# Two attention decodes on one core: the value loads and output weights of the full-cache part move from the SP queue to the Activation queue

## The chip, the cores and the metric

The kernel runs on one core of one Trainium2 chip. The metric is the device time of one execution in microseconds. Times of a kernel are medians of its timed runs; each profile is of one execution, and its span is 1 to 2 us below the time of that execution.

## The reference, cut to what matters

Two decode attentions for the same batch of 4, one query token each, joined on the last axis. A is grouped (32 query heads, 8 key heads) over the last 2048 positions of its cache. B, the "full-cache part", is plain multi-head over all 8192 positions.

```python
def _B_ref(x, k_cache, v_cache, wq, wo):           # k_cache, v_cache: [4, 32, 8192, 128] bf16
    q = (x @ wq).reshape(B, 1, 32, 128).transpose(0, 2, 1, 3)
    scores = einsum("bhqd,bhkd->bhqk", q, k_cache) * 128 ** -0.5
    o = einsum("bhqk,bhkd->bhqd", softmax(scores), v_cache)
    return o.transpose(0, 2, 1, 3).reshape(B, 1, 4096) @ wo
```

B reads 2 x 268 MB of cache once. All the inputs read are 587 MB.

## The kernel before

B is cut into 64 chunks of two heads of one batch entry. A chunk has 4 MB of keys and 4 MB of values; each lands as 128 rows of 32 KB, one for each partition. Keys and values have two buffers each (the last values have one more). For each chunk, TensorE transposes the keys in 16 groups of 8 tiles; VectorE, or in every third group ScalarE (the Activation engine), copies a group from PSUM to SBUF; TensorE multiplies by the query. The value part of the chunk before comes behind the keys of a chunk. Output weights of B (`wos`) are 256 KB in 128 rows of 2 KB, one load for every four chunks.

```python
def keys_part(c):
    for g in range(ch["NG"]):                      # 16 groups
        emit_T(ch["s"] + g)                        # 8 transposes, then a copy on ScalarE if g % 3 == 2
        if g >= SLAG:
            emit_S(ch["s"] + g - SLAG)             # scores
        # [...] at g == 10 of odd chunks: emit_fin, which reads wos and frees it
for c in range(NC):
    # [...]
    keys_part(c)
    values_part(c - 1, c)                          # [...] values of c-1; max and exp of c
```

All big loads stand in one list on the SP queue: keys of chunk c+1, values of c, keys of c+2, and so on. Each waits for its buffer: keys for the last transposes of two chunks earlier, values for the value part of two chunks earlier.

```python
for kind, c in loads:
    if kind == "k" and c >= NCA and (c == NCA or (c - NCA) % 4 == 3 and c > NCA + 3):
        dma_wos((c - NCA) // 4)
    dma_kv(kind, c)
    # [...]
```

The engines' streams are recorded first. Repeated stretches on TensorE, VectorE and ScalarE become loops, if their instructions are the same.

## Time and profile before

| | before |
|---|---|
| median of the timed runs | 1374.2 us (1374.04 to 1374.27) |
| span of the profiled execution | 1372.6 us |
| data moved, mean rate | 587.53 MB, 428 GB/s |
| TensorE busy | 86% |

Three more lines are from the page's list of loads: out<-in, queue, count, size of one, and the median time from issue to landing.

```profile
kv<-in_B_k_cache_dram SPq DMA_DIRECT2D x63, 4096.0 KB, 26.5
kv<-in_B_v_cache_dram SPq DMA_DIRECT2D x63, 4096.0 KB, 30.9
...
wos<-in_B_wo_dram SPq DMA_DIRECT2D x16, 256.0 KB, 20.3
```

Keys and values both land some three load times (9.7 us each) after their issue: the queue is always about three loads deep.

### The profile page before, as it was taken

The numbers are of one execution on the slowest core, as the hardware profiler recorded it, in microseconds if no ns is written. First come the engines' busy times: TensorE is split into PE (matmuls) and PEld (weight loads), VectorE is DVE, ScalarE is ACT, GpSimd is POOL, SyncE is SP. The second block draws the span as 40 slices with busy tenths as digits, with TensorE's granted clock in tenths as the row PEclk, the third lists the DMA queues.
The fourth block names the chain that finished last, engine by engine and source line by source line (L and its number), as shares of the span: only waits on it lengthen the run. The fifth ranks groups of instructions, "written<-read, shape, count | busy, mean of one in ns | idle before, by whom it ended". The sixth has DMA issues, their size and how long they took to land.

```text
span 1372.6 us, 59967 instructions
## 1 busy us (share of the span) xinstructions
PE 1176.5 (86%) x27065; PEld 1132.9 (83%) x27067; DVE 656.6 (48%) x1434; ACT 434.7 (32%) x650; POOL 7.3 (1%) x28
## 2 busy tenths in 40 slices
PE   4888898889888888988888888888898888888888
PEld 4777898888888888888888878888898888888888
DVE  1775454445444444454445444444454444444544
ACT  1553232333223322332233323322333233323322
POOL 2000000000000000000000000000000000000000
PEclk9998999999999999999999999999999999999999
DMA  9999999999999999999999999999999999999998
GB/s 400 423 424 432 429 433 428 433 432 432 432 431 433 429 434 428 434 430 434 430 434 430 430 433 432 432 431 433 429 433 431 434 429 434 430 432 432 432 427 352
DMA packets 25261, 587.53 MB, mean 428 GB/s; under 512 B 2820, under 2 KB 2840, under 8 KB 6296
## 3 DMA queue, kind: packets, MB, share of 16 engines
q1 hardware_dynamic: 25208, 587.22, 99.8%
q8 instruction: 16, 0.26, 0.1%
q14 instruction: 5, 0.04, 0.0%
q10 hardware_dynamic: 32, 0.01, 0.0%
HBM read 587.21 MB, written 0.01 MB: 428 GB/s over the span
## 4 chain that ended last, share of the span: by engine, by line
DMA 65%; PE 33%; issue 1%; DVE 1%; ACT 0%; SPq 0%; DVEq 0%
DMA kv<-in_B_k_cache_dram 57%; PE tr L408 21%; PE sc L410 9%; DMA kv<-in_A_k_cache_dram 5%; DMA kv<-in_B_v_cache_dram 3%; PE po L410 2%; PE fin L410 1%; PE ms L410 0%; ACT kt L476 0%; DVE sA L527 0%; SPq L365 0%; ACT pba L597 0%; PE ms L408 0%; DVE zA L683 0%; DVE rm L536 0%
## 5 line engine op out<-in xcount | busy, mean ns | idle before, releaser
L408 PE MATMUL tr<-identb,kv 128*128 128x128 bf16 x8704 | 697.9, 230 | 148.8 <-DMA kv<-in_B_k_cache_dram 141.5
L478 DVE COPY kt<-tr 128x1024 bf16<-128x1024 bf16 x736 | 502.6, 690 | 457.1 <-PE tr L408 452.7
L408 PEld LDWEIGHTS tr<-identb,kv 128*128 128x128 bf16 x8704 | 552.9, 104 | 165.2 <-DMA kv<-in_B_k_cache_dram 81.7
L476 ACT ACTIVATE kt<-tr 128x1024 bf16<-128x1024 bf16 x352 | 359.3, 1023 | 666.8 <-PE tr L408 666.7
L410 PE MATMUL sc<-qb,kt 128*128 128x64 bf16 x8704 | 446.2, 196 | 14.3 <-ACT kt L476 12.8
L410 PEld LDWEIGHTS sc<-qb,kt 128*128 128x128 bf16 x8704 | 366.4, 100 | 26.0 <-ACT kt L476 20.2
L410 PE MATMUL po<-pbb,kv 128*128 128x64 bf16 x8320 | 284.4, 192 | 4.5 <-issue 3.9
L410 PEld LDWEIGHTS po<-pbb,kv 128*128 128x128 bf16 x8320 | 263.2, 97 | 7.1 <-issue 4.1
L577 ACT ACTIVATE pbb<-sc,negb 64x128 bf16<-64x128 f32 x128 | 51.6, 403 | 254.3 <-DVE negb L564 253.5
L541 DVE TENSOR_REDUCE rm<-sc 64x1 f32<-64x128 f32 x128 | 37.0, 289 | 56.6 <-PE sc L410 55.7
L553 DVE TENSOR_REDUCE gm<-ms 1x2 f32<-1x128 f32 (+1 forms) x72 | 20.1, 279 | 48.4 <-PE ms L408 48.4
L564 DVE COPY negb<-ms 128x1 f32<-128x1 f32 (+1 forms) x72 | 11.4, 158 | 47.0 <-PE ms L410 46.8
L410 PE MATMUL ms<-identf,gx 1*128 1x1 f32 (+1 forms) x144 | 27.2, 256 | 0.8 <-DVE zA L683 0.8
L666 DVE TENSOR_TENSOR oz<-po,rz 128x8 bf16<-128x8 f32 x33 | 5.5, 166 | 40.7 <-PE po L410 40.7
L410 PEld LDWEIGHTS ms<-identf,gx 1*128 1x128 f32 (+1 forms) x144 | 21.1, 182 | 4.6 <-DVE zA L683 0.9
L577 ACT ACTIVATION_READ_ACCUMULATOR pbb<-sc,negb 64x1 f32 x128 | 23.7, 185 | 0.0
L410 PE MATMUL po<-pba,kv 128*128 128x64 bf16 x512 | 20.5, 199 | 3.5 <-issue 2.1
L410 PEld LDWEIGHTS po<-pba,kv 128*128 128x128 bf16 x512 | 17.9, 102 | 5.7 <-ACT pba L597 4.2
L408 PE MATMUL ms<-identf,rm 128*1 128x128 f32 (+1 forms) x72 | 19.5, 271 | 2.4 <-DVE rm L536 2.3
L557 DVE TENSOR_SCALAR gx<-gm 1x128 f32<-1x128 f32 (+1 forms) x72 | 16.0, 222 | 2.5
L683 DVE CAST zB<-ms 64x8 bf16<-64x8 f32 x64 | 10.5, 164 | 9.2 <-PE ms L410 8.7
L410 PE MATMUL ms<-xT,kv 128*128 128x4 bf16 x256 | 7.1, 166 | 8.8 <-DMA kv<-in_A_wq_dram 5.0
(61 smaller groups left out, 173.9 us busy)
## 6 DMA issues: line engine op xcount, KB each, us to landing
kv<-in_B_k_cache_dram SPq DMA_DIRECT2D x63, 4096.0 KB, 26.5
kv<-in_B_v_cache_dram SPq DMA_DIRECT2D x63, 4096.0 KB, 30.9
kv<-in_A_k_cache_dram SPq DMA_DIRECT2D x8, 2048.0 KB, 14.8
kv<-in_A_v_cache_dram SPq DMA_DIRECT2D x8, 2048.0 KB, 16.2
kv<-in_A_wq_dram SPq DMA_DIRECT2D x1, 4096.0 KB, 12.5
kv<-in_B_wq_dram SPq DMA_DIRECT2D x1, 4096.0 KB, 27.1
wor<-in_A_wo_dram SPq DMA_DIRECT2D x8, 512.0 KB, 9.8
wos<-in_B_wo_dram SPq DMA_DIRECT2D x16, 256.0 KB, 20.3
```

What stands on the lines that cost most here:

```text
L408: sch.add("pe", lambda e: e.transpose(o, l, r), waits, key)
L410: sch.add("pe", lambda e: e.matmul(o, l, r, start=start, stop=stop), waits, key)
L476: sch.add("act", lambda e: e.activation(dst, src, ACTF.Copy), waits=waits, key=("ev", s))
L478: sch.add("dve", lambda e: e.tensor_copy(dst, src), waits=waits, key=("ev", s))
L541: sch.add("dve", lambda e, src=src, pp=pp: e.tensor_reduce(out=rm[pp, m, 0:1], in_=src, axis=AX.X, op=ALU.max), waits=[("S", ch["s_last"]) ...
L553: sch.add("dve", lambda e: e.tensor_reduce(out=gm[0:C, m, 0:U], in_=src, axis=AX.X, op=ALU.max), waits=[("trm", c)], key=("gmax", c))
L557: sch.add("dve", lambda e: e.tensor_scalar(out=dst, in0=gv, scalar1=-scale, scalar2=None, op0=ALU.mult), waits=[("gmax", c)], key=("gx", c))
L564: sch.add("dve", lambda e: e.tensor_copy(negb[:, m, 0:C], ms[:, col:col + C]), waits=[("bc", c)], key=("negb", c))
L577: sch.add("act", lambda e, src=src, pp=pp, n=n, u=u: e.activation(probs_of(c)[pp, :, u], src, ACTF.Exp, bias=negb[pp, m, 0:1], scale=scale ...
L666: sch.add("dve", lambda e: e.tensor_tensor(out=o, in0=i0, in1=i1, op=ALU.mult), waits=waits, key=("oT", c))
L683: sch.add("dve", lambda e, src=src, pp=pp: e.tensor_copy(z[pp, :].rearrange("p (r b) -> p r b", r=k), src), waits=[("sm", c)] + free if h ...
```

## The change

The intent is to take values and weights out of the list on SP, so that neither kind waits behind the other's buffer. Values are issued by the Activation engine between its copies: ahead of group 11 of the same chunk's keys (group 2 for the last chunk), with the weights ahead of them in every fourth chunk.

```diff
-            sch.add_dma("sp", lambda e: e.dma_start(wos[...], src), "d_wos",
+            sch.add_dma(VQ if hp else "sp", lambda e: e.dma_start(wos[...], src), "d_wos",
[...]
-            sch.add_dma("sp", lambda e: e.dma_start(dst, src), "d_h%d" % at, waits=waits, key=(kind, c))
+            sch.add_dma("sp" if kind == "k" else VQ, lambda e: e.dma_start(dst, src), "d_h%d" % at, waits=waits, key=(kind, c))
+
+        def dma_values(c):
+            if c > NCA + 3 and (c - NCA) % 4 == 1:
+                dma_wos((c - NCA) // 4)
+            dma_kv("v", c)
[...]
         for kind, c in loads:
-            if kind == "k" and c >= NCA and (c == NCA or (c - NCA) % 4 == 3 and c > NCA + 3):
-                dma_wos((c - NCA) // 4)
-            dma_kv(kind, c)
+            if kind == "k" and c == NCA:
+                dma_wos(0)
+            if kind == "k" or c < NCA:
+                dma_kv(kind, c)
[...]
             for g in range(ch["NG"]):
+                if c >= NCA and g == (11 if c < NC - 1 else 2):
+                    dma_values(c)
                 emit_T(ch["s"] + g)
```

`VQ` is "act". The last values' five pieces move in the same way.

More of the change, by code (lines that the diff above doesn't have):

```diff
@@ L14 @@
 TG = 8
+VQ = "act"
 NTRB = 3
@@ L339, in dma_wos @@
             src = B_wo[2 * hp * P:2 * (hp + 1) * P, :].rearrange("(p r) n -> p (r n)", r=2)
-            sch.add_dma("sp", lambda e: e.dma_start(wos[:, :, :].rearrange("p r n -> p (r n)"), src), "d_wos",
+            sch.add_dma(VQ if hp else "sp", lambda e: e.dma_start(wos[:, :, :].rearrange("p r n -> p (r n)"), src), "d_wos",
                         waits=[("fin", NCA + 4 * hp - 1)] if hp else [], key=("wos", hp))
@@ L364, in dma_kv @@
                     x = slice(j0 * P, (j0 + n) * P)
-                    sch.add_dma("sp", lambda e, x=x: e.dma_start(dst[:, x], src[:, x]), "d_vl%d" % i, waits=waits, key=("vl", j0))
+                    sch.add_dma(VQ, lambda e, x=x: e.dma_start(dst[:, x], src[:, x]), "d_vl%d" % i, waits=waits, key=("vl", j0))
                     j0 += n
@@ L373, in dma_kv, with say_landed @@
                 return
-            sch.add_dma("sp", lambda e: e.dma_start(dst, src), "d_h%d" % at, waits=waits, key=(kind, c))
+            sch.add_dma("sp" if kind == "k" else VQ, lambda e: e.dma_start(dst, src), "d_h%d" % at, waits=waits, key=(kind, c))
[3 more added lines that the diff above has]
+            dma_kv("v", c)
+        def say_landed(c):
+            hp = max(0, c - NCA - 2) // 4
+            sch.add("sp", lambda e: e.sem_inc(sems["eng_sp"], 1), waits=[("wos", hp)] + (["kl"] if c == NC - 1 else []),
+                    key=("wos2", c - 2 if c > NCA + 1 else NONE), self_inc=True)
         dma_x(0)
@@ L387, in bass_concat_heads__sliding_block_cached__mha_block_cached__decode_kernel @@
         for kind, c in loads:
-            if kind == "k" and c >= NCA and (c == NCA or (c - NCA) % 4 == 3 and c > NCA + 3):
-                dma_wos((c - NCA) // 4)
-            dma_kv(kind, c)
-            if kind == "v" and c > NCA and (c - NCA) % 2 == 1:
-                hp = max(0, c - NCA - 2) // 4
-                sch.add("sp", lambda e: e.sem_inc(sems["eng_sp"], 1), waits=[("wos", hp)] + (["kl"] if c == NC - 1 else []),
-                        key=("wos2", c - 2 if c > NCA + 1 else NONE), self_inc=True)
+            if kind == "k" and c == NCA:
+                dma_wos(0)
+            if kind == "k" or c < NCA:
+                dma_kv(kind, c)
+            if kind == "k" and c > NCA + 1 and (c - NCA) % 2 == 0:
+                say_landed(c - 1)
             if kind == "v" and c < NCA:
                 dma_wo(c)
+        say_landed(NC - 1)
         sch.add("sp", lambda e: e.sem_inc(sems["eng_sp"], 1), waits=[("wos", HB // 2 - 1)], key=("wos2", NC - 1), self_inc=True)
```

## The prediction

> **What bounds the kernel now.** I read the page from the top (busy shares, slices, queues), then the chain of waits in order of time, the table of waits, the issue times on the SP queue, and last the end of the timeline.
>
> ```profile
> span 1372.6 us, 59967 instructions
> PE 1176.5 (86%) x27065; PEld 1132.9 (83%) x27067; DVE 656.6 (48%) x1434; ACT 434.7 (32%) x650; POOL 7.3 (1%) x28
> DMA  9999999999999999999999999999999999999998
> GB/s 400 423 424 432 429 433 428 433 432 432 432 431 433 429 434 428 434 430 434 430 434 430 430 433 432 432 431 433 429 433 431 434 429 434 430 432 432 432 427 352
> DMA packets 25261, 587.53 MB, mean 428 GB/s; under 512 B 2820, under 2 KB 2840, under 8 KB 6296
> ```
>
> The reader is to see that the DMA engines are busy in every slice and that the rate is flat: 587.53 MB at 432 GB/s take 1360 us of the 1372.6. TensorE comes close behind and is not the bound.
>
> ```profile
> 380.11 28.58 DMA kv<-in_B_k_cache_dram
> 408.75 1.51 PE tr L408 x24
> 414.67 0.47 PE tr L408 x8
> 416.36 0.55 PE tr L408 x8
> 419.67 27.89 DMA kv<-in_B_k_cache_dram
> 447.60 1.51 PE tr L408 x24
> ...
> PE tr L408 <- DMA kv<-in_B_k_cache_dram: 141.5, 58, 4.1
> ...
> PE po L410 <- DMA kv<-in_B_v_cache_dram: 0.7, 2, 0.5
> ```
>
> The chain alternates: a key load is issued when the transposes of two chunks earlier have freed its buffer, lands 28 to 29 us later, and starts the next transposes. 4.19 MB alone need 9.7 us at 432 GB/s, so some 19 us of other loads lie ahead of it in the queue. TensorE waits for keys (141.5 us) and almost never for values (0.7 us). In the chain, keys of every second chunk start at 212.43 and, 28 steps on, at 1309.89: 39.2 us for two chunks. Two chunks load four times 4.194 MB and half of a 0.262 MB weight load, 16.91 MB, which is 431 GB/s. In this part the time is bytes over that rate.
>
> ```profile
> 602.58 0.33 SPq L374 DMA_DIRECT2D kv<-in_B_v_cache_dram  x1
> 612.02 0.33 SPq L340 DMA_DIRECT2D wos<-in_B_wo_dram  x1
> 615.29 0.33 SPq L374 DMA_DIRECT2D kv<-in_B_k_cache_dram  x1
> 620.63 0.33 SPq L374 DMA_DIRECT2D kv<-in_B_v_cache_dram  x1
> ...
> 1347.01 1.51 PE L408 MATMUL tr<-identb,kv 128*128 128x128 bf16 x24
> ...
> 1369.11 0.41 PE L410 MATMUL po<-pbb,kv 128*128 128x64 bf16 x8 [0.23 <-DMA kv<-in_B_v_cache_dram]
> ```
>
> These are columns start and duration. An issue costs its queue 0.33 us. In the chunk whose keys start at 604.37, the transposes end at 615.3 (the key issue follows at once), the value part ends at 620.6 (so the value issue), and the next keys start at 623.87: 10.9 + 5.3 us of work, 3.3 us of wait. In the next chunk the tensor clock starts low and the transposes take 13.4 us. The last two lines matter for the tail: the last chunk's keys start at 1347.01, right behind the work before, and the last value piece holds TensorE up for 0.23 us only. The last loads and the last compute end together; 25.6 us run from 1347.0 to the end.
>
> **What the Trainium skill says.** "DMA: Bandwidth & Descriptors", section "Issuing engines are not separate DMA queues": loads issued on several engines run on the same 16 DMA engines and interleave, and only issue time is saved. The trace agrees as far as it can: 79 loads move, at 0.33 us each, and the issuing SP queue bounds nothing. The same page, "Specifications", gives a fabric ceiling of 435 GB/s; the 431 measured is 0.9% below. The same page, "Queues, rings and completion order": each DMA engine goes round-robin between the queue rows, a packet at a time. No run shows yet how these 32 KB rows share. "Runtime: NRT & Kernel Launch", section "Instruction fetch mechanics": instructions come in 16 KiB blocks that are fetched ahead, mostly hidden; the trace shows a queue of 16 such packets, 0.26 MB in all.
>
> **The change part by part.**
> 1. *Bytes*: none added or removed. At the unchanged rate the 1097 us of steady state stay.
> 2. *Issue*: 64 value chunks (the last in five pieces) and 15 weight loads leave SP for the Activation engine's in-order stream, at 0.33 us: 83 x 0.33 = 27 us over the span on an engine that is 32% busy. In most chunks they stand between the copy that starts at +5.7 us of the keys and the one at +8.2 us, a gap of 1.0 to 1.5 us in the trace. The value buffer has long been free by then, so it does not wait. On the path: nothing.
> 3. *The loop of the Activation stream*: the order of instructions shows it unrolled (311 rows for 65), since a load names another address each time. PE and DVE keep their loops, row for row. The extra instruction blocks are some 0.1 MB by my estimate, under 0.3 us at 431 GB/s, fetched ahead. On the path: about nothing.
> 4. *When values are issued*: before, as the value part frees the buffer (602.58, 1.8 us ahead of the keys at 604.37). After, behind the third Activation copy of the keys, which ends at 611.1: 8.5 us later; in the slow-clock chunk (620.63 to some 633.6) 13 us later. A value load then has from +6.7 us to the next-but-one start of values at 19.6 + 10.9 = +30.5, that is 24 us, or in the slow-clock case 21. Alone it needs 9.7; at half the rate beside the keys 19.5 plus a landing time of 1 to 2 us. So it fits with 0 to 3 us to spare. I expect TensorE to wait for values for the first time, a few us in some chunks, in exchange for a shorter wait for keys. No byte moves slower for that: at the start of a chunk's keys, the next keys (9.7 us of work) are already queued on SP, more than the 6.7 us until values come. DMA stays full, and the 39.2 us stand. I add 1 us for spots near 130 to 190 us, where the pipeline fills.
> 5. *The tail*: before, keys went wholly ahead of the values behind them. Sharing brings keys later in relation to bytes. Take s, when the second-last chunk's keys start. The loads still to come then: about 6 us of the values before it, then 9.7 each for the last keys, the second-last values and the last values: 35 us. The trace has DMA finishing near 1369, so s is near 1334 (it was 1329.4). The last keys share for 19.5 us and land at 1353.5; with the 25.6 us from there the end is 1379.1, or 6.5 us beyond 1372.6. The last values are now issued behind the exponentials of the second-last chunk, near s + 18, with other values still queued, so DMA does not run dry.
> 6. *Load boundaries*: the steady 39.2 us are 0.34 us over 16.91 MB at 435.2 GB/s, about 85 ns for each of four loads. In the first part, with smaller loads, the slices show 424. If each load's end leaves a short hole, a second queue can fill it: at most 0.34 us x 32 pairs = 11 us. I count a quarter, 3 us, as the trace does not show the holes themselves.
>
> Sum: 0 + 0 + 0 + 1 + 6.5 - 3 = +4.5 us, so 1374.2 + 4.5 = about 1378.5 us.
>
> **The rivals.**
> - *The second queue raises the rate.* For: 431 against 435, and the lower rate with smaller loads. Against: packet time already fills 99.8% of the engines. With all 11 us gained and the full tail loss: 1370; without tail loss: 1363.
> - *Values become the bound and DMA runs dry.* For: the late issue with 0 to 3 us to spare, and a weight load of 2 KB rows taking turns with 32 KB rows could hold a value load up several us every fourth chunk. Against: dry needs both queues empty at once. If 1 us were lost per pair, 32 us: 1410.
> - *Sharing goes load by load, not row by row.* Then keys and values alternate as before, values still arrive in time, and the tail does not move: 1374, or 1371 with point 6.
> - *Switching between two streams costs rate.* Nothing in the trace speaks for it; 1% would be 12 us: 1390.
> - *Activation stalls hold up the copies.* Even 1 us per chunk would be hidden in the 1.3 to 3.3 us that TensorE waits; no effect.
>
> **Range and chances.** The sum is 1378.5; full gain at the boundaries brings 1367, moderate drying or switching 1391. Faster by over 2% needs under 1346.7, below the 1350 that all the bytes take at 435 GB/s: 1%. Slower by over 2% needs over 1401.7, the drying rival nearly in full: 5%. Within 2%: 94%.
>
> **What would show it.** Point 1: GB/s of the slices from 430 to 434. Point 2: 0.33 us per issue on the Activation queue and no longer copies. Point 4: time to landing of values near 20 us (31 before) and of keys near 28 still, a new wait of TensorE for values of tens of us in sum, and the wait for keys down from 141.5. Point 5: the last keys starting near 1353 instead of 1347, and DMA done near 1369, some 9 us before the end. Point 6: 39.2 us per pair falling to 39.1. I am wrong if the slices of the steady part change by over 1%, if values land as before, or if the tail does not grow.

## The result, and the profile after

The changed kernel takes 1393.4 us (median of 4, 1389.4 to 1395.9) against 1374.2 us. The ratio is 1.0137 (95% interval 1.0112 to 1.0163). Here and below, a ratio is the mean time of one kernel's fast runs over that of the other's of the same rounds, so not quite the ratio of the medians quoted. It is 1.4% slower, inside the 2% that was held likely, but above the range of 1367 to 1391. The runs of before agree within 0.3 us, those of the change scatter over 6.5 us. The profiled execution is the fastest of the four (1389.4), so what the trace shows is 15.1 us of a median loss of 19.2.

First the page after, top to bottom: span, rate in 40 slices, the two queues (q1 is SP's, q10 is the Activation queue's), the list of loads; then two lines of the waits.

```profile
span 1387.7 us, 59487 instructions
...
GB/s 399 424 425 430 407 437 432 429 431 433 433 431 422 433 426 432 423 424 438 402 431 428 425 424 432 432 428 431 415 435 427 431 421 429 435 414 433 416 430 311
...
q1 hardware_dynamic: 13256, 314.84, 52.9%
q10 hardware_dynamic: 11984, 272.39, 46.2%
...
kv<-in_B_k_cache_dram SPq DMA_DIRECT2D x63, 4096.0 KB, 23.1
kv<-in_B_v_cache_dram ACTq DMA_DIRECT2D x63, 4096.0 KB, 24.0
...
PE po L422 <- DMA kv<-in_B_v_cache_dram: 165.6, 31, 12.4
...
PE tr L420 <- DMA kv<-in_B_k_cache_dram: 12.7, 11, 2.6
```

The rate is no longer flat: slices of 402 to 425 stand among the 430s. And the waits have changed sides: TensorE waited 141.5 us for keys and 0.7 for values, and now 12.7 for keys and 165.6 for values, up to 12.4 us at once.

One such wait, from the timeline after (start, duration, engine, line; in brackets the idle time before and what ended it):

```profile
619.17 0.33 ACTq L341 DMA_DIRECT2D wos<-in_B_wo_dram  x1
619.53 0.46 ACTq L375 DMA_DIRECT2D kv<-in_B_v_cache_dram  x1
...
634.55 0.34 ACTq L375 DMA_DIRECT2D kv<-in_B_v_cache_dram  x1
...
652.26 1.04 PE L422 MATMUL po<-pbb,kv 128*128 128x64 bf16 x16 [12.15 <-DMA kv<-in_B_v_cache_dram]
...
658.82 1.50 PE L420 MATMUL tr<-identb,kv 128*128 128x128 bf16 x24
...
664.51 0.34 ACTq L375 DMA_DIRECT2D kv<-in_B_v_cache_dram  x1
...
669.73 0.33 SPq L375 DMA_DIRECT2D kv<-in_B_k_cache_dram  x1
```

Weights are issued at 619.17 and values right behind them. These values take 32.7 us to land, and TensorE waits 12.15 us for them. Meanwhile keys go on landing. Then comes what costs time. The next keys start at 658.82, the values of that chunk are issued only at 664.51, and further keys only at 669.73, when the transposes have freed their buffer. Here is what DMA did in the same stretch (window, its length, busy time of PE, PEld, DVE, ACT and POOL, granted clock, DMA share, GB/s):

```profile
661.00:663.00 2.00, 2.00 (x52) 2.00 (x50) 1.37 (x2) 0.92 (x2) 0.00 (x0) 1.00 1.10 475
663.00:665.00 2.00, 2.00 (x52) 2.00 (x50) 1.57 (x4) 0.98 (x2) 0.00 (x0) 1.00 0.20 82
665.00:667.00 2.00, 2.00 (x47) 1.73 (x45) 1.50 (x3) 0.53 (x1) 0.00 (x0) 1.00 1.00 279
667.00:669.00 2.00, 2.00 (x53) 2.00 (x50) 1.30 (x2) 1.02 (x1) 0.00 (x0) 1.00 1.10 475
```

By the packet records, 14 of the 16 DMA engines end the last row that was issued to them between 663.6 and 664.6; two still have rows of the values before, up to 666.3. The rest stands still until the rows of the issue at 664.51: they start at 665.5 and take about 2 us (median 1.96, 1.5 to 2.3) instead of 1.21, and full rate is back at 667. Such dry spells stand in the packet records at intervals of some 80 us, that is four chunks, or one weight load: eleven from 427 to 1298 us, with 15 weight loads. The one shown is the deepest; in the others only a part of the engines runs out. In the mean of the 16 engines, 5.4 us more than before pass without a row (124 to 1355 us), and the 32 KB rows of the whole run take 6.5 us more, above all just behind dry spells (197 rows over 1.4 us after 124 us, 10 before). The two together are about the loss of DMA time given below. From the chain after, keys of a chunk start at 373.61, and those of 48 chunks later at 1325.63: 79.3 us for four chunks, against 78.4 before.

How weights hold values up can be read from the packet records, too. They do not name the DMA engine, but one engine's packets follow each other without a gap, so they can be strung together. This is the order on three of the 16 engines from 619 to 652 us, the first of them much as on most of the others (K: a 32 KB row of keys, V: a 32 KB row of values, w: a 2 KB row of weights, small letters k, v: end of a load on the SP, Activation queue):

```
most engines:       V K v K w K w k w w w w w w v V K V K V K V K V K V K V K V K v k V K V K V K V
one engine behind:  K V K v K w K w K w k w K w K w K w K w K v K V K V K V k V V K V K V K V K v K V
another behind:     K V K v K w K w k w w w K w K w K w K v K V K V K V K V k V V K V K V K v K V K
```

The two queues take strict turns, row by row, whatever the size of a row. On most engines the keys' load ended (k) while the weights were passing, so six weight rows passed in one go. On two engines the order was different: each weight row of 84 ns waited for a key row of 1.21 us. The values behind the weights started there at 632.7 and 634.8, on the others at about 625, and ended at 649.6 and 651.7, on the others at 643.0 to 645.2. TensorE wanted them from 640.1 and got them at 652.26, after the slowest engine. So some 7 of its 12 us of wait come from the two slow engines; by the others the values would still have been about 5 us late.

The loss splits in two, by the end of the last load's last row in the packet records:

| | last row lands | from there to the end | span |
|---|---|---|---|
| before | 1368.6 | 4.0 | 1372.6 |
| after | 1380.0 | 7.7 | 1387.7 |

So 11.4 us were lost by DMA on the way and 3.7 us in the tail. Of the 11.4, 1.6 us are lost by the time 70 MB have been moved (168 us), where B begins; the rest comes in the steps described.

### The profile page after: what moved, and what is told of

It reads as the page before. It is cut to its first block, busy times and chain, and to the rows that moved or that the text cites. A ratio compares the mean times of both kernels' runs of the same rounds, so it can differ in the third digit from the quotient of the medians.

```text
span 1387.7 us, 59487 instructions
## 1 busy us (share of the span) xinstructions
PE 1153.6 (83%) x27065; PEld 1104.8 (80%) x27067; DVE 654.1 (47%) x1434; ACT 435.1 (31%) x650; POOL 7.4 (1%) x28
## 4 chain that ended last, share of the span: by engine, by line
DMA 56%; PE 40%; ACT 1%; issue 1%; DVE 1%; ACTq 0%; SPq 0%; DVEq 0%
DMA kv<-in_B_v_cache_dram 33%; DMA kv<-in_B_k_cache_dram 19%; PE tr L420 18%; PE po L422 10%; PE sc L422 9%; DMA kv<-in_A_k_cache_dram 2%; DMA kv<-in_B_wq_dram 2%; PE ms L422 1%; PE fin L422 1%; ACT kt L488 1%; PE ms L420 0%; ACTq L341 0%; DVE sA L539 0%; DVE rm L548 0%; ACT pba L609 0%
## 5 line engine op out<-in xcount | busy, mean ns | idle before, releaser
L420 PE MATMUL tr<-identb,kv 128*128 128x128 bf16 x8704 | 650.5, 221 | 18.2 <-DMA kv<-in_B_k_cache_dram 12.7
L420 PEld LDWEIGHTS tr<-identb,kv 128*128 128x128 bf16 x8704 | 510.3, 99 | 31.8 <-DMA kv<-in_B_k_cache_dram 13.3
L422 PE MATMUL po<-pbb,kv 128*128 128x64 bf16 x8320 | 309.5, 198 | 171.9 <-DMA kv<-in_B_v_cache_dram 165.6
L422 PE MATMUL sc<-qb,kt 128*128 128x64 bf16 x8704 | 436.9, 194 | 14.7 <-ACT kt L488 13.0
L422 PEld LDWEIGHTS po<-pbb,kv 128*128 128x128 bf16 x8320 | 287.1, 101 | 178.3 <-DMA kv<-in_B_v_cache_dram 169.3
L422 PEld LDWEIGHTS sc<-qb,kt 128*128 128x128 bf16 x8704 | 353.8, 99 | 29.7 <-ACT kt L488 24.2
L576 DVE COPY negb<-ms 128x1 f32<-128x1 f32 (+1 forms) x72 | 11.4, 159 | 52.6 <-PE ms L422 52.6
## 6 DMA issues: line engine op xcount, KB each, us to landing
kv<-in_B_k_cache_dram SPq DMA_DIRECT2D x63, 4096.0 KB, 23.1
kv<-in_A_wq_dram SPq DMA_DIRECT2D x1, 4096.0 KB, 12.4
```

The lines of the kernel that those rows point to most:

```text
L420: sch.add("pe", lambda e: e.transpose(o, l, r), waits, key)
L422: sch.add("pe", lambda e: e.matmul(o, l, r, start=start, stop=stop), waits, key)
L576: sch.add("dve", lambda e: e.tensor_copy(negb[:, m, 0:C], ms[:, col:col + C]), waits=[("bc", c)], key=("negb", c))
```

## The experiments

Three theories at first: W: weights ahead of values on the same queue hold values up. L: late issue (group 11) by itself lets DMA run dry. S: two streams as such cost rate. Later ones concern the tail (T). All kernels gave correct results. Times are medians of 4 (before: 1374.1 to 1374.3). All edits are against the changed kernel, unless said otherwise.

### Weights back on SP

```diff
-            sch.add_dma(VQ if hp else "sp", ..., "d_wos",
+            sch.add_dma("sp", ..., "d_wos",
```
and issued at the place in the list where before has them.

> The change as it is, but the weight loads of the full-cache part (15 of 256 KB in 2 KB rows) go back to the SP queue at the place they had before; values stay on the Activation queue, issued as late as in the change. Theory W (the weight load stands ahead of a value load on the same queue, makes it land some 10 us late in every fourth chunk, and DMA runs dry after it): the 10 to 12 us waits of TensorE for values go, DMA stays full, what is left is the tail of 4 to 5 us: 1376 to 1381 us. Theory L (late issue at half the rate is enough by itself to run dry, weights or not): 1388 us or more, with waits for values spread over all chunks. Theory S (two streams cost rate as such): 1388 or more and no value waits over 5 us.

Measured: 1386.0 us, ratio 1.0088 (1.0071 to 1.0105). The long waits for values are gone, and the rate is 431 GB/s from 200 to 1200 us (428 in the change). Waits, and two windows, of this run:

```profile
PE tr L418 <- DMA kv<-in_B_k_cache_dram: 125.0, 41, 8.0
...
200.00:700.00 500.00, 433.53 (x10008) 419.29 (x10005) 237.70 (x501) 155.57 (x230) 0.00 (x0) 0.93 1.00 431
...
1370.00:1375.00 5.00, 5.00 (x153) 4.87 (x150) 1.35 (x6) 0.91 (x4) 0.00 (x0) 1.00 0.04 15
```

The total is above what W expected, for another reason: the last row lands at 1372.0, 3.4 us later than before, but 10.8 us pass from there to the end (4.0 before). From 1370 on DMA has nothing to do, and TensorE is still busy. Its last keys started at 1354.1 (1347.0 before), late against the end of the loads. So the steady part speaks for W, and the tail has become larger than in the change.

### Weights on a queue of their own

```diff
-            sch.add_dma(VQ if hp else "sp", ..., "d_wos",
+            sch.add_dma("pool", ..., "d_wos",
```

> The change as it is, but the weight loads are issued by GpSimd on a queue of their own, at the same waits, so they stand ahead of neither values nor keys. Theory W: 1376 to 1381 us, value loads land in 21 to 25 us in every chunk, no value wait over 4 us. Theory L: 1388 us or more. Theory S: 1388 or more. If here it is fast and with the weights on SP it is not, it is the 2 KB rows between 32 KB rows of any loaded queue that hurt.

Measured: 1384.0 us, ratio 1.0075 (1.0058 to 1.0092). As in the run before: the longest wait for values is 3.2 us, the last row lands at 1371.6, and the tail is 10.3 us. The time misses the range expected by the same tail; the values' landing (median 26.4 us) is a little above it.

### Values early

```diff
-                if c >= NCA and g == (11 if c < NC - 1 else 2):
-                    dma_values(c)
+                if c >= NCA and g == 2:
+                    dma_kv("v", c)
+                if c > NCA + 3 and (c - NCA) % 4 == 1 and g == 11:
+                    dma_wos((c - NCA) // 4)
```

> Weights stay on the Activation queue at group 11 of the chunk, but the value load is issued at group 2 of the chunk's keys, about 8 us earlier (so behind the exponentials of the chunk before, and the weights now stand between two value loads). Theory L: issue time is the whole matter, so 1376 to 1380. Theory W: the weights still hold up the next value load on some engines, but it has 8 us more until it is needed, so most of the loss goes too: 1376 to 1383, with waits for values behind weights of 0 to 4 us instead of 10 to 12. Theory S: 1388 or more.

Measured: 1376.4 us, ratio 1.0020 (1.0003 to 1.0036). The time is as expected. The reason is not the one that W gave, as TensorE's waits for values are still there:

```profile
PE po L422 <- DMA kv<-in_B_v_cache_dram: 134.2, 38, 12.2
...
668.20 1.04 PE L422 MATMUL po<-pbb,kv 128*128 128x64 bf16 x16 [12.23 <-DMA kv<-in_B_v_cache_dram]
```

Values behind weights come 12 us late, TensorE waits, and it costs nothing, as DMA is never without work: the packet records show no dry spell from 124 to 1355 us. The last row lands at 1369.0, 0.4 us later than before, though all B data came over two queues. That rules S out, and it also says that a second queue wins no rate.

### Both

Values at group 2, weights on GpSimd's queue.

> Both: values issued at group 2, weights on the GpSimd queue. All that theories W and L blame is gone: steady part as before, tail 4 to 5 us longer: 1376 to 1379 us. Theory S (two streams cost rate as such): 1385 or more, with DMA busy throughout.

Measured: 1382.5 us, ratio 1.0059 (1.0042 to 1.0076): slower than the run with early values alone, which was not expected. The difference is all in the tail: the last row lands at 1369.5, and 11.4 us follow (5.6 with early values alone). The waits say why:

```profile
PE tr L420 <- DMA kv<-in_B_k_cache_dram: 143.0, 59, 4.4
```

Here TensorE waits for keys throughout and not at all for values; keys share the rate with values that could come later, so the last keys come late (they start at 1355.2, with early values alone at 1350.4). With weights on the value queue, values are late and keys are ahead, and the tail is short in most of those runs. That this is the reason is argued, not shown: the next run has its weights there and a long tail.

### A small load ahead of every value load, values late and early

```diff
             if c > NCA + 3 and (c - NCA) % 4 == 1:
                 dma_wos((c - NCA) // 4)
+            elif c < NC - 1:
+                sch.add_dma(VQ, lambda e: e.dma_start(dose[:, :], B_wo[0:P, 0:256]), "d_dose", [...])
             dma_kv("v", c)
```

> The change as it is, and one more small load (64 KB, 128 rows of 512 B, into a tile that nobody reads) on the Activation queue ahead of each of the 48 value loads that have no weights before them. Its own packets cost at most 48 x 8 rows x 30 ns = 12 us. Theory W+L (small rows on the value queue take turns one for one with 32 KB key rows and hold values up; with the late issue DMA then runs dry): the hold-up now comes in every chunk, so more than the 12 us: 1410 to 1440 us, with TensorE waiting for values in most chunks and the rate of the slices below 425. If small rows ahead of values are harmless, at most 1393 + 12 = 1405.

Measured: 1396.7 us, ratio 1.0155 (1.0138 to 1.0172). The expectation of W and L together (1410 or more) is missed: this is only 3 us over the change, less than the packets of the small loads cost by themselves (384 rows for each engine, 27 ns each, 10 us). TensorE does wait for values in 47 chunks, 159.3 us in sum, but dry spells are no more frequent than in the change. So the loss does not count hold-ups. One reading is that a hold-up in every chunk keeps the value queue always behind and seldom empty, and that the loss needs one followed by a stretch in which TensorE and the queues catch up; no run tests that.

The same with values and small loads at group 2, on top of that (the weights are taken out of `dma_values`, which is not shown, and issued at group 11):

```diff
-                if c >= NCA and g == (11 if c < NC - 1 else 2):
+                if c >= NCA and g == 2:
                     dma_values(c)                # small load, then values
+                if c > NCA + 3 and (c - NCA) % 4 == 1 and g == 11:
+                    dma_wos((c - NCA) // 4)
```

> The same small loads ahead of values, but values (and small loads) issued at group 2, as in the run with early values. Theory W+L: values still land late, but they have 8 us more, so DMA does not run dry and only the packets of the small loads (at most 12 us) are added to 1376: 1380 to 1390 us. If the hold-up costs DMA time by itself, as much over 1376 as the other dose run is over 1393.

Measured: 1386.2 us, ratio 1.0088 (1.0071 to 1.0105), 10 us over the run with early values. That is what the packets of the small loads cost, as expected; hold-ups add nothing that can be seen.

### The last two values behind the last keys

On top of the run with weights on SP: the last two value loads go on SP behind the last keys, as in before.

```diff
+        def last_values():                       # called in the last chunk, all keys being listed by then
+            dma_kv("v", NC - 2)                  # both on "sp"
+            dma_kv("v", NC - 1)
[...]
-                if c >= NCA and g == (11 if c < NC - 1 else 2):
+                if NCA <= c < NC - 2 and g == 11:
                     dma_values(c)
+                if c == NC - 1 and g == 2:
+                    last_values()
```

> The run with the weights on SP (1386 us), and the last two value loads also on SP behind the last keys, as in the kernel before; all other values on the Activation queue, issued late. Theory T (in that run what is left of the loss is 2.5 us where the full-cache part begins and 7 us in the tail, because sharing brings the last keys late): the tail goes, 1377 to 1379 us. If the tail is not the order of the last loads: 1384 or more.

Measured: 1382.0 us, ratio 1.0053 (1.0036 to 1.0069). The tail falls from 10.8 to 6.0 us, which speaks for T. The total does not fall as much. In the profiled execution, the slowest of the four, DMA lost more on the way (last row at 1376.7 instead of 1372.0; dry spells near 350 and 1215 us) although the two kernels are the same up to the last chunks. Its timed runs range from 1379.9 to 1384.4. So with late values and weights on SP dry spells can occur too, and it seems that they differ from one execution to the next.

With values at group 2 on top of that:

```diff
-                if NCA <= c < NC - 2 and g == 11:
+                if NCA <= c < NC - 2 and g == 2:
                     dma_values(c)
```

> The same, and values issued at group 2 instead of 11, so nothing is left of what the theories blame: late issue, weights ahead of values, last keys behind shared bandwidth. Two queues otherwise as in the change. Theory: the same as the kernel before within 2 us: 1373 to 1376. If two streams cost rate as such, 1380 or more.

Measured: 1383.2 us, ratio 1.0057 (1.0041 to 1.0074). The expectation is missed clearly. The weights are now on the key queue, and there they hold keys up: strung together from 548 to 586 us, most of the eight weight rows wait for a value row each, on all the engines, before keys go on. TensorE waits up to 12.5 us for keys (158.3 us in all), the last row lands at 1373.4, and the tail is 9.6 us. Weights on either loaded queue hold up what shares that queue, so this kernel was not free of what the theories blame. The long tail with the last values behind the last keys is no support for T.

### Early values, with the last two values behind the last keys

> The run with early values (weights on the Activation queue, 1376.4 us), and the last two value loads on SP behind the last keys, as in the kernel before. Theory T (what was left there is the order of the last loads): 1374 to 1375.5 us. If nothing is left to win at the end: 1376 to 1377.

On the run with early values (weights on the Activation queue):

```diff
-                if c >= NCA and g == 2:
+                if NCA <= c < NC - 2 and g == 2:
                     dma_kv("v", c)
+                if c == NC - 1 and g == 2:
+                    last_values()                # the last two, on "sp" behind the last keys
```

Measured: 1376.4 us, ratio 1.0014 (0.9998 to 1.0031). No gain: the tail is 5.5 us (5.6 without). There keys were ahead already (the last ones start at 1350.4 in both), so T may have had nothing to mend in this kernel.

### Values at group 5

```diff
-                if c >= NCA and g == 2:
+                if c >= NCA and g == (5 if c < NC - 1 else 2):
```
(against early values)

> The run with early values, with values issued at group 5 instead of 2, that is behind the first Activation copy of the chunk, some 3 us into its keys; weights as there, at group 11 behind the values. Theory L (DMA runs dry between the landing of what is queued and the issue at group 11): the dry spell shrinks with the delay, so nearly all of the gain stays: 1375 to 1380 us. If only the order of weights and values matters: as the next run.

Measured: 1376.7 us, ratio 1.0022 (1.0005 to 1.0039), last row at 1369.3, no dry spell, values waited for by 134.0 us. As expected: some 3 us into the keys is early enough.

### Values at group 11, weights behind them

```diff
-                if c >= NCA and g == 2:
+                if c >= NCA and g == (11 if c < NC - 1 else 2):
```
(against early values; so the change with the two issues swapped)

> The change as it is, but at group 11 the value load is issued first and the weights behind it: values as late as in the change, weights no longer ahead of the values that are needed next. Theory W+L (the dry spell needs a hold-up by weights and the late issue): the hold-up moves to the value load of the next chunk, which is issued 20 us later, so it is mostly gone: 1378 to 1386 us, with the tail of 3 to 7 us and the start of 2 us left. Theory L alone: as the change, 1390 to 1396.

Measured: 1387.3 us, ratio 1.0097 (1.0079 to 1.0116), just above the range. The tail is 4.6 us, but the last row lands at 1379.1, nearly as late as in the change. Waits for values still reach 12.2 us and sum to 152.3:

```profile
PE po L422 <- DMA kv<-in_B_v_cache_dram: 152.3, 33, 12.2
```

So the order of weights and values within a chunk is the smaller part: 6 us of the median, and in the profiled executions 0.9 us of DMA time and 3.1 of the tail. Weights anywhere on the value queue hold some value load up, and with the late issue DMA runs dry. Between this run and the one with early values only the group of the value issue differs (11 or 2): that is 10.1 us of DMA time (1379.1 against 1369.0).

### Late issue on one queue

Against the kernel before, all loads on SP:

```diff
+            if kind == "v" and NCA <= c < NC - 1:
+                waits = waits + [("ev", ch["s"] + 8)]   # the third Activation copy of the chunk
```

> The kernel before with all loads on SP, but each value load of the full-cache part also waits for the third Activation copy of its chunk, so it is issued as late as in the change, on one queue. Theory (the loss needs a second queue that takes turns): loads still land in the order of issue and keys cannot run ahead of values, so 1374 to 1377 us. If late issue as such runs DMA dry: 1385 or more.

Measured: 1376.3 us, ratio 1.0014 (0.9997 to 1.0031), as expected. Two windows and two waits of this run:

```profile
120.00:160.00 40.00, 35.34 (x763) 33.48 (x761) 19.92 (x45) 11.16 (x15) 0.00 (x0) 0.91 0.96 404
...
200.00:700.00 500.00, 431.66 (x9999) 419.42 (x9996) 237.47 (x499) 155.03 (x230) 0.00 (x0) 0.94 1.00 431
...
PE tr L410 <- DMA kv<-in_B_k_cache_dram: 145.1, 59, 4.1
...
PE po L412 <- DMA kv<-in_B_v_cache_dram: 0.7, 2, 0.5
```

Late issue costs 3.5 us of DMA time where B begins (404 GB/s from 120 to 160 us, the last row at 1372.1) and nothing after that. On one queue keys cannot run ahead of values: waits are as in before, and the tail is 4.0 us as in before.

### The twelve together

| kernel | median us | last row lands | tail | longest wait for values |
|---|---|---|---|---|
| before | 1374.2 | 1368.6 | 4.0 | 0.5 |
| the change | 1393.4 | 1380.0 | 7.7 | 12.4 |
| weights on SP | 1386.0 | 1372.0 | 10.8 | 2.8 |
| weights on GpSimd's queue | 1384.0 | 1371.6 | 10.3 | 3.2 |
| values early | 1376.4 | 1369.0 | 5.6 | 12.2 |
| values early, weights on GpSimd's queue | 1382.5 | 1369.5 | 11.4 | none |
| small loads, late | 1396.7 | 1385.0 | 11.0 | 10.0 |
| small loads, early | 1386.2 | 1380.1 | 5.3 | 5.3 |
| weights on SP, last values on SP | 1382.0 | 1376.7 | 6.0 | 3.3 |
| the same, early | 1383.2 | 1373.4 | 9.6 | none |
| values early, last values on SP | 1376.4 | 1369.1 | 5.5 | 12.4 |
| values at group 5 | 1376.7 | 1369.3 | 4.7 | 11.9 |
| group 11, weights behind | 1387.3 | 1379.1 | 4.6 | 12.2 |
| one queue, late | 1376.3 | 1372.1 | 4.0 | 0.5 |

Last row, tail and wait are of the one profiled execution, the median of all; where the timed runs scatter, the two do not belong together. The profiled execution was the slowest of four for both runs with small loads, both with weights and last values on SP, and one queue, late; it was the fastest for the change. (The small loads' own packets are part of the last row's time in those two.) No version beats the kernel before, and reordering loads could not by much: before keeps DMA full up to 1368.6 us.

## Why the prediction was right or wrong, point by point

- *Bytes and issue (points 1 and 2): right.* The median 32 KB row takes 1.21 to 1.22 us in both kernels, and an issue takes 0.33 to 0.46 us of the Activation queue. The rival of a stalled Activation engine had no effect either: it is held up at the 15 weight loads (27.0 us in sum), but TensorE waits no longer for its copies (13.0 us against 12.8).
- *The unrolled Activation stream (point 3): right as far as seen.* Of the two instruction queues one moved 0.26 MB before and after, the other 0.04 and 0.07 MB, so less than the 0.1 MB estimated was added; and the run with early values, whose stream is unrolled too, loses 0.4 us of DMA time.
- *When values are issued (point 4): the step that failed.* It expected a value load to fit "with 0 to 3 us to spare" and TensorE to wait for values "a few us in some chunks"; the waits came, larger (165.6 us in sum, 12.4 the longest). Values took 24.0 us to land (near 20 expected), keys 23.1 (near 28). It concluded: "No byte moves slower for that [...] DMA stays full, and the 39.2 us stand. I add 1 us". The argument was that at the start of a chunk's keys the next keys are still queued, 9.7 us of work against 6.7 us until values come. After a long wait for values less is left of them, as keys go on landing: in the example most engines ran out 5 to 6 us after the keys' start at 658.82, and the first value rows came 6.7 us after it. Measured in its place: 11.4 us of DMA time, 1.6 of them at the start of B and the rest in dry spells behind weight loads. The rival "values become the bound and DMA runs dry" had named the parts (a late issue, and "a weight load of 2 KB rows taking turns with 32 KB rows"), and was given little weight because both queues must be empty at once. They are, on some or most of the DMA engines, once for most weight loads. That two things must meet, late issue and small rows on one of two loaded queues, is shown: the run with values early keeps the hold-up and has no dry spell; with weights on a queue of their own the late issue stays and the last row lands at 1371.6; late issue on one queue has no loss in the steady part. With weights on the key queue the late issue went well in one profiled execution (1372.0) and less well in another (1376.7).
- *The tail (point 5): it grew, but its reason is only in part shown.* 6.5 us were predicted and 3.7 came. The last keys start at 1362.9 us (near 1353 expected) and DMA is done at 1380.0 (near 1369), both late by about what DMA had lost. That the hold-up by weights puts keys ahead and so shortens the tail is argued. With all values on the Activation queue and weights on another, the tail grew by 6.3 to 7.4 us (10.3, 10.8 and 11.4 against 4.0), near the 6.5. Moving the last values behind the last keys took 4.8 us of it in one run and nothing in another; the late small loads have a tail of 11.0 that nothing here explains.
- *Load boundaries (point 6): wrong.* 3 us of gain were counted, none came: with early values the last row lands 0.4 us later than before. The lower rate with smaller loads goes with a cost of each row: rows of 2, 4, 16 and 32 KB take 84, 159, 613 and 1214 to 1216 ns in the packet records (medians), some 9 to 13 ns more than bytes over one fixed rate.
- *The sum:* 1 + 6.5 - 3 = 4.5 us were predicted; the trace has 11.4 + 3.7 + 0 = 15.1 us. The median is 4 us beyond that again. Those slower executions were not profiled, so where they lose more is open; that dry spells depend on which engines are behind would explain a scatter, but this is only argued. Open, too, is why some DMA engines are behind the others when weights come.

## What to carry to other kernels

With DMA already full, the second queue had no rate to give here; it only changed the order in which loads land, and that order was good. Before splitting a queue, ask which load is needed first at each point, above all at the end, and what a load of small rows will do to the loads behind it on its queue. If loads are split, issue each as soon as its buffer is free: with values early, waits of TensorE of up to 12.2 us cost 0.4 us of DMA time, as loads were queued all along; with values late, waits of the same length went with 11.4. Moving the small rows to a queue of their own was no gain on top of that (1382.5 us against 1376.4).

## What the Trainium skill lacked or had wrong

- "DMA: Bandwidth & Descriptors", section "Issuing engines are not separate DMA queues": more issuing engines "will only save the time on the sequencer". The runs agree that no rate is won (last row at 1369.0 against 1368.6 us), but the page does not say that it can cost: 1.4% here, as loads landed in another order and DMA ran dry.
- The same page, "Queues, rings and completion order": the switch between rows comes at packets of some 9 to 17 descriptors. In these traces two loaded queues alternate after every single row of 32 KB, and a 2 KB row takes a turn like a 32 KB row (84 ns against 1.21 us), so that with 256 KB ahead of it a load ended 5 to 7 us later on two engines of 16 than on the others.
- The same page, "Specifications", has a first-byte latency of about 0.6 us for loads issued from this engine, and the trace does not speak against it: after the standstill the first rows start at 665.48 us, 1.0 us after the start of the issue (664.51) and 0.6 after its end. What no page was found to say is that rows then take longer for a while: about 2 us instead of 1.21, which over the whole run (6.5 us) cost as much as the standstills themselves (5.4 us).
